# Sliding-window attention and a token-mixing MLP on one core: a new order of the work, six output buffers, first pieces in two parts, last stores tile by tile

## The chip, the cores and the metric

The kernel runs on one core of a Trainium2 chip. The metric is the device time of one execution in microseconds; the profiled execution also has a span, from its first to its last instruction. Engines are named PE (TensorE), DVE (VectorE), ACT (ScalarE), POOL (GpSimd) and SP (SyncE, which here only issues DMAs).

## What is computed

Attention over 576 positions with a window of 128, a linear position bias of its own for each of 8 heads, for 8 batches; its output then passes through a mixing layer, in which the tokens of a batch are mixed by a product of two projections:

```python
q, k, v: (8, 8, 576, 64)                      # batch, head, position, 64
scores = q @ k.T / 8 - slope[h] * |i - j|     # only 0 <= i - j < 128
x = softmax(scores) @ v                       # heads side by side: (8, 576, 512)
W_tok = (x @ w_q) @ (x @ w_k).T / 8           # (8, 576, 576)
out = relu(W_tok @ x) @ w_out                 # (8, 576, 512) float32
```

## The kernel before, in words

Everything is cut into some 735 small operations, and each is given an engine, PSUM banks and a place by one long list, `PLAN` (line 99). An item such as `36A0` is operation 36 on ACT with PSUM bank 0; P is PE, D is DVE, G is POOL, S is SP. `planned` (line 81) reads it. Every engine works through its own operations in exactly this order, so an operation that waits holds up all behind it on its engine. The list is written into the code; costs and due times given to each `op` are those that its planner used, and have no effect when the kernel runs.

The operations of a batch b, by name:

- `ld q`/`ld k` (two halves f of four heads each), `ld v` (five blocks of positions, the last one of 64): loads of 576 KB, 256 KB and 128 KB in float32, issued by SP (lines 392 and 427).
- `cast` (line 396, 431): float32 to float16, mostly on POOL; in batch 0 also on DVE and ACT. Each cast on POOL is made to wait for the last bias product M that stands before it in the list (the dependency named "port", line 698).
- `T` (line 399): 18 transposes of 64 x 64 on PE, then `evac` (line 408), which copies the result from PSUM to qT or kT, on ACT or DVE.
- `S` (line 445) and `E` (line 459): for a pair of heads c and a half u, the score products and their exponential (ACT, 128 x 1024). `M` (line 471, DVE) multiplies by the table of exponentials of the bias, zero outside the window.
- `PV` (line 488): 18 products with v, then `NR` (reciprocal) and `N` (scaling) on DVE, which write x.
- `XT`/`XTe` (lines 523, 534): 18 transposes of x and two copies; `WK`/`WKe`, `WQ`/`WQe`: the two projections and their copies; `G`/`Ge`: x weighted by one projection, summed over tokens, and its copy; `MX` (line 593) and `R` (line 600): the product with the other projection, and relu with the scale, written by two instructions to rm and rmt.
- `O` (line 623): four products with w_out for 128 positions, `Oe` (line 629) copies the result to an output buffer osb, and `st` (line 638) stores two such tiles, 512 KB. The last 64 positions of two batches go together: `OT`, `OTe` and `stt`, with buffers osbt.

In names such as S101 or O63 the first digit is the batch. Buffers are reused in rings whose lengths stand in `RINGS` (line 145): 8 for loads, 6 for casts of q and k, 3 for osb, 2 for osbt. The weights w_out and w_q, w_k are loaded through osb and osbt too (line 359).

At the start POOL and DVE make the identity, the masks and pads; ACT makes eight exponentials for the bias, DVE spreads them into a table (`table`, line 349). Nine operations `warm` (line 337) of four products of a matrix of ones with itself run on PE, into PSUM banks that nothing reads: eight of them first, and the ninth in batch 1.

Before the change, the early orders are (SP, ACT, PE, and DVE, cut):

```
SP   k00 q00 k01 q01 k10 v04 q10 v03 v01 v00 v02 k11 q11 w2 w3 k21 k20 v10 v14 q21 v11 v12 v13 q20
ACT  8 exps, cast k00, cast q00, evac q00, E011 E000 E001 E010 E031, cast v04, E030, evac q10, E021 E020, cast v02, E101 E100, evac q11, evac k11
DVE  table0 table1, evac k00 k01 q01, M00, evac k10, cast v03, M01 M03, cast v00 v01, M02, NR00 N00
PE   8 warm, T k00, T q00, S011, T k01, S001 S000, T q01, S010, T k10, S031 S021 S030 S020, T q10, PV00 PV01 S101 S100 PV02 PV03, T k11, T q11
end of PE   XT71 O61 XT73 O60 WK7 WQ7 G7 O62 MX72 MX71 MX70 MX73 O63 O72 O73 O71 O70 OT3
```

Of the kernel before, what the change touches and what calls it, by code (L numbers as in the profile page):

```python
# [9 lines left out]
FP32 = mybir.dt.float32  # L10
# [5 lines left out]
P = 128  # L16
# [16 lines left out]
class Op:  # L33
# [3 lines left out]
    def __init__(self, engs, name, prio, fn, reads=(), writes=(), after=(), opens=None, psum=None,  # L37
                 mode="F", dma=0.0, lag=0.0):
        self.engs, self.name, self.prio, self.fn = engs, name, prio, fn
        self.reads, self.writes, self.after = list(reads), list(writes), list(after)  # L40
        self.opens, self.psum, self.mode, self.dma, self.lag = opens, psum, mode, dma, lag
        self.deps, self.room, self.memory = {}, set(), {}
        self.banks = self.eng = self.place = None
        self.insts = []


def link(ops, rings):
# [4 lines left out]
    for o in ops:  # L52
        for r in o.writes:
            writers.setdefault(r, []).append(o)
        for r in o.reads:
            readers.setdefault(r, []).append(o)
# [24 lines left out]
def planned(ops):  # L81
# [3 lines left out]
    for item in PLAN.split():  # L85
# [4 lines left out]
        if o.opens:  # L90
# [9 lines left out]
1G 6D 39S 4D 0G 35S 2D 7D 47S 3G 8P0 5D 43S 14P0 20A 65S 19A 11P0 23A 59S 18A 12P0 17A 61S 24A 25D  # L100
21A 9P0 57S 22A 40A 15P0 53S 26D 13P0 51S 10P0 55S 36A 41P2 73S 42D2 69S 37P0 31S 38A0 48G 33S
250P0 99S 49P2 251A0 44G 245P4 91S 50D2 243P6 77S 244A6 45P0 248P2 66G 46D0 246A4 249A2 67P6 247D
260P0 255P4 261A0 258P2 62G 68D6 60A 253P0 259A2 58D 63P6 252D 64A6 256A4 262D 254A0 52D 54D 56A
257D 85S 403P0 95S 406P2 79S 404D0 74G 405D0 265P4 81S 263P6 266A4 407D2 83S 408D2 411P0 70G 87S
264A6 414P4 412D0 413D0 117S 75P2 32G 71P6 29S 415D4 34G 409P0 416D4 72A6 27S 410D0 113S 417P4
76A2 268P6 100G 418D4 270P0 269A6 280P2 267D 101P4 281A2 273P6 92G 102D4 274A6 531P2 78G 271A0
532D2 278P6 93P4 86G 275P2 279A6 272D 535P0 94A4 96G 533P1 536D0 276A2 534D1 80G 537P4 539P0 277D
111S 97P2 538A4 16P6 125S 98A2 82G 540D0 109S 84G 105S 282D 103S 427P0 419P2 107S 88G 428D0 121S
295P4 420D2 429D0 422P6 296A4 143S 421D2 293P0 118G 89P4 294A0 423D6 424D6 430P2 90A4 431D2 30G
541P0 425P6 432D2 542A0 283P4 426D6 433P2 284A4 28G 288P0 434D2 285P6 286A6 297D 290P4 547P2 289A0  # L110
543P6 287D 545P3 544A6 300P0 114G 546D3 291A4 119P6 548D2 549P3 120D6 301A0 126G 298P4 550A3 115P0
292D 127P6 299A4 650P2 110G 128D6 116A0 645P3 106G 651A2 112G 137S 557P0 646D3 553P4 104G 643P2
139S 554A4 558D0 133S 108G 644A2 135S 302D 435P0 131S 438P2 129S 122G 436D0 310P4 439D2 440D2
648P6 147S 311A4 647S 437D0 303P2 144G 649A6 123P4 304A2 124D4 138G 145P0 446P6 146A0 308P2 140G
447D6 448D6 443P4 309A2 555P0 444D4 441P6 134G 445D4 556A0 141P2 142A2 442D6 449P0 305P4 136G
450D0 306A4 551P6 313P2 552D6 559P0 314A2 132G 307D 315P4 163S 318P6 316A4 320P2 157S 655P1 130G
560D0 151S 319A6 451P4 159S 321A2 663P0 148G 195S 452D4 453D4 177S 323P6 664A0 312D 325P2 165S
149P4 656A1 161S 563P0 324A6 322D 169S 326A2 561P1 155S 317D 652S 454P6 564A0 462P2 150A4 164G
455D6 562D1 653P0 463D2 152G 456D6 459P4 654A0 464D2 660P1 160G 657S 460D4 158G 461D4 173S 153P2
661A1 328P6 189S 154D2 658P0 329A6 196G 203S 330P4 191S 659D0 565P6 333P2 331A4 199S 566D6 178G  # L120
457P0 334A2 465P4 458D0 197P6 466D4 198A6 338P0 166G 571P2 572D2 340P4 339A0 573P6 327D 341A4
575P7 162G 574D6 335P0 569P2 567P4 336A0 170G 577P6 568D4 570A2 576D7 156G 179P0 578D6 167P2 180A0
171P4 332D 467P6 168A2 666P0 337D 172A4 668P1 468D6 469D6 470P2 667A0 669A1 579P4 471D2 581P6
472D2 174G 580A4 673P0 670S 582A6 662S 585P2 342D 175P4 185S 586A2 345P6 671P1 346A6 183S 190G
674D0 181S 478P2 204G 176A4 672D1 187S 348P6 479D2 207S 480D2 475P0 349A6 192G 350P4 476D0 583P2
477D0 351A4 473P6 200G 474D6 481P0 584A2 343P4 482D0 344A4 353P6 355P2 352D 587P0 356A2 683P1
588D0 354A6 347D 678P0 684A1 186G 193P2 679A0 358P4 194D2 360P6 359A4 591P0 184G 361A6 357D 215S
201P2 205P4 209S 202A2 589P1 182G 592D0 221S 681P6 590D1 206A4 217S 188G 211S 362D 491P0 682A6
233S 483P2 225S 492D0 486P4 484D2 216G 493D0 676P6 208G 487D4 485D2 686P7 210G 677A6 488D4 680S
597P0 687A7 370P2 598D0 213S 494P4 371A2 222G 675S 593P6 495D4 373P0 594A6 496D4 241S 489P2 374A0  # L130
229S 380P6 490D2 218G 497P4 665S 498D4 381A6 223P2 375P0 212G 224D2 365P4 237S 376A0 601P6 235S
366A4 603P7 602D6 685S 377D 363P0 239S 599P2 368P4 364A0 605P6 600D2 226G 369A4 604D7 595P0 606D6
234G 227P2 596A0 219P4 372D 378P6 220A4 696P0 214G 228D2 379A6 694P1 697A0 367D 613P4 607P2 609P6
608A2 689P0 610A6 382D 507P2 614A4 691P6 690A0 242G 508D2 509D2 695A1 499P4 230G 692A6 611P0 500D4
383P2 501D4 612A0 693S 502P6 384A2 688S 238G 231P0 503D6 504D6 510P4 232A0 698S 709P2 236G 511D4
512D4 385P0 505P6 386A0 400P4 506D6 701P3 401A4 710D2 240G 398P0 702D3 513P6 711S 399A0 393P4
514D6 699P2 394A4 402D 615P3 700A2 395P0 616D3 388P4 703S 396A0 390P6 387D 617P2 389A4 619P3 618D2
397D 391A6 515P0 706P2 620A3 516D0 392D 621P4 625P6 622A4 704P3 517D0 707A2 626D6 518P4 705A3
627P0 519D4 708S 523P6 520D4 628A0 623P2 524D6 526P0 624A2 525D6 521P4 527D0 528D0 714P2 522D4
529P0 715A2 712P3 530D0 629P2 713D3 631P0 630D2 716S 633P1 632D0 717P0 634A1 639P2 637P4 635P6  # L140
640A2 638D4 641P2 636D6 719P1 642A2 718D0 727P2 720D1 729P3 728A2 721S 724P2 730A3 731S 722P3
725A2 732P2 723A3 726S 733A2 734S
# [3 lines left out]
         "wkn": 2, "wqT": 2, "g": 2, "rm": 8, "rmt": 8, "osb": 3, "osbt": 2, "inv": 3}  # L146
# [96 lines left out]
def steps(nc, pool, pp, q, k, v, moe_w_q, moe_w_k, moe_w_out, out):  # L243
# [24 lines left out]
    osb = [sb([P, 2, DM], FP32, f"osb{i}") for i in range(3)]  # L268
    osbt = [sb([P, DM], FP32, f"osbt{i}") for i in range(2)]
# [65 lines left out]

    for i in range(9):
        def f_warm(eng, bk):
            for _ in range(4):
                nc.tensor.matmul(bank(bk[0])[:, 0:P], ones, ones, start=True, stop=True)
        op({"PE": 0.45}, f"warm{i}", -98 + i, f_warm, reads=[("ident", 0)],  # L340
           opens=(f"warm{i}", 1))

# [31 lines left out]
    for i in range(4):  # L374
        r = [("osb", i - 3) if i < 2 else ("osbt", i - 4)]
        op({"SP": 0.6}, f"ld w{i}", (20, 20, 8, 8)[i], lambda eng, bk, i=i: f_ldw(eng, bk, i),
           writes=r, dma=1.4 if i < 2 else 0.7)
        op({"POOL": 1.04 if i < 2 else 0.33}, f"cast w{i}", (24, 24, 12, 12)[i],
           lambda eng, bk, i=i: f_castw(eng, bk, i), reads=r, writes=[("w", i)])
# [5 lines left out]
    for b in range(NB):  # L385
        for f in range(2):
            for x in range(2):
# [26 lines left out]
                op({"SP": 0.6}, "ld " + name, base - 14, f_load, writes=[("ld", i)], dma=1.65)  # L414
                op({"POOL": 1.12} if b else {"POOL": 1.12, "DVE": 1.15, "ACT": 1.0},
# [25 lines left out]
    for b in range(NB):  # L441
        for c in range(4):
            base, n = b * PERIOD + c * SLOT, 4 * b + c
            for u in range(2):
# [14 lines left out]
                def f_exp(eng, bk, n=n, u=u):  # L459
# [6 lines left out]
                   reads=[("qT", 2 * b + c // 2), ("kT", 2 * b + c // 2)],  # L466
# [13 lines left out]
    for b in range(NB):  # L480
        for c in range(4):
# [61 lines left out]
            op({"DVE": 0.74}, f"XTe{b}{c}", prio + 2.0, f_xte, psum=key,  # L543
# [3 lines left out]
    for b in range(NB):  # L547
# [35 lines left out]
        op({"DVE": 0.41}, f"WKe{b}", base + 3.0, f_wke, psum=f"WK{b}", writes=[("wkn", b)])  # L583
        op({"PE": 0.56}, f"WQ{b}", base + 4.0, f_wq, reads=r_xT + [("w", 2)],
           opens=(f"WQ{b}", 1), mode="C")
        op({"DVE": 0.41}, f"WQe{b}", base + 4.5, f_wqe, psum=f"WQ{b}", writes=[("wqT", b)])
# [31 lines left out]
    for b in range(NB):  # L618
        base = b * PERIOD + 6 * SLOT
        for t in range(4):  # L620
            n = (b * 4 + t) // 2

            def f_out(eng, bk, b=b, t=t):
                for db in range(4):
                    r = slice(256 * (t // 2) + t % 2, 256 * (t // 2) + 256, 2)
                    nc.tensor.matmul(bank(bk[0]), rm[:, b % 2, db, r],
                                     wout_sb[:, db, :], start=(db == 0), stop=(db == 3))

            def f_oute(eng, bk, t=t, n=n):
                copy(eng, osb[n % 3][:, t % 2, :], bank(bk[0]))  # L630
# [5 lines left out]
               writes=[("osb", n)])  # L636
            if t % 2:
                def f_store(eng, bk, b=b, t=t, n=n):
                    nc.sync.dma_start(
                        out=out[b, P * (t - 1) : P * (t + 1), :].rearrange("(p t) d -> p t d", t=2),  # L640
                        in_=osb[n % 3])
                op({"SP": 0.6}, f"st{b}{t}", base + t * SLOT + 1.6, f_store, dma=1.45,
                   reads=[("osb", n)])
        if b % 2:
# [7 lines left out]
            def f_outte(eng, bk, pr=pr):  # L652
                copy(eng, osbt[pr % 2], bank(bk[0]))

            def f_storet(eng, bk, pr=pr):
                for i in range(2):
                    nc.sync.dma_start(out=out[2 * pr + i, 512:576, :],
                                      in_=osbt[pr % 2][64 * i : 64 * i + 64])
# [72 lines left out]
```

## Time and profile before

| | |
|---|---|
| time, median of 4 runs | 150.74 us (149.59 to 152.04) |
| time of the profiled execution | 150.81 us |
| its span | 149.1 us |
| busy: PE, DVE, ACT, POOL | 125.4, 125.5, 118.5, 58.7 us |
| one exponential (64 of them, ACT) | 1.036 us |
| one bias product M (32, DVE) | 1.293 us |
| one cast of a q or k piece on POOL | 1.146 us |
| one copy of a q or k piece from PSUM: ACT, DVE | 1.12 and 1.36 us |
| one copy of an O tile: ACT, DVE | 0.606 and 0.685 us |
| from issue to landing: 512 KB store, 128 KB store | 4.3 and 3.2 us (median) |
| bytes moved by DMA | 39.4 MB |

Busy time says how much work an engine has; a stretch in which no engine is nearly always busy is one in which in-order queues wait for one another. A matmul's time in the records is its passage through the array; matmuls overlap, so a row of several is shorter than the sum of its parts. The list of idle times before a group names what came last.

### The profile page before, as it was taken

The numbers are of one execution on the slowest core, as the hardware profiler recorded it, in microseconds if no ns is written. First come the engines' busy times: TensorE is split into PE (matmuls) and PEld (weight loads), VectorE is DVE, ScalarE is ACT, GpSimd is POOL, SyncE is SP. The second block draws the span as 40 slices with busy tenths as digits, with TensorE's granted clock in tenths as the row PEclk, the third lists the DMA queues.
The fourth block names the chain that finished last, engine by engine and source line by source line (L and its number), as shares of the span: only waits on it lengthen the run. The fifth ranks groups of instructions, "written<-read, shape, count | busy, mean of one in ns | idle before, by whom it ended". The sixth has DMA issues, their size and how long they took to land.

```text
span 149.1 us, 5314 instructions
## 1 busy us (share of the span) xinstructions
PE 125.4 (84%) x2308; PEld 81.8 (55%) x2308; DVE 125.5 (84%) x212; ACT 118.5 (79%) x170; POOL 58.7 (39%) x78
## 2 busy tenths in 40 slices
PE   6568368776889968989989998999899999999870
PEld 6445266555756446647466566566644757555320
DVE  5739987979999996979999989999999989994700
ACT  6958947995889868997699999968999989741560
POOL 4054236454826756433936372365342710000000
PEclk9999968999999999999999999999999999999999
DMA  4999999999997999999999999589999975033075
GB/s 140 390 347 256 230 323 350 252 181 349 394 286 157 298 284 228 298 291 327 349 361 321 345 390 239 129 232 318 299 359 288 328 257 190 4 141 145 0 316 176
DMA packets 50775, 39.40 MB, mean 264 GB/s; under 512 B 39488, under 2 KB 39488, under 8 KB 50752
## 3 DMA queue, kind: packets, MB, share of 16 engines
q1 hardware_dynamic: 50752, 39.07, 88.9%
q8 instruction: 18, 0.29, 0.8%
q14 instruction: 5, 0.04, 0.1%
HBM read 29.62 MB, written 9.44 MB: 262 GB/s over the span
## 4 chain that ended last, share of the span: by engine, by line
PE 51%; DVE 21%; ACT 14%; DMA 6%; POOL 2%; SPq 1%; issue 1%; DVEq 0%; POOLq 0%
PE bank L159 51%; ACT pt L159 8%; DMA ld<-in_k_dram 6%; DVE pt L159 5%; DVE x L159 4%; DVE xT L159 3%; DVE kT L159 3%; POOL nat L159 2%; ACT qT L159 2%; ACT kT L159 2%; DVE osb L159 1%; SPq L159 1%; DVE rm L159 1%; DVE qT L159 1%; ACT rm L159 1%
## 5 line engine op out<-in xcount | busy, mean ns | idle before, releaser
L159 ACT ACTIVATE pt<-bank 128x1024 f16<-128x1024 f32 x64 | 62.7, 1036 | 9.2 <-PE bank L159 8.8
L159 POOL CAST nat<-ld 128x1152 f16<-128x1152 f32 x30 | 34.1, 1146 | 34.1 <-PE bank L159 12.4
L159 DVE TENSOR_TENSOR pt<-pt,table 128x2048 f16<-128x2048 f16 x32 | 40.9, 1293 | 1.5 <-ACT pt L159 1.5
L159 PE MATMUL bank<-wout_sb,rm 128*128 128x512 f16 x128 | 31.8, 380 | 0.0
L159 POOL CAST vt<-ldv 128x512 f16<-128x512 f32 (+1 forms) x35 | 20.8, 613 | 24.9 <-DVE pt L159 15.0
L159 PE MATMUL bank<-qT,kT 64*128 64x256 f16 (+2 forms) x320 | 25.5, 268 | 3.8 <-ACT qT L159 1.5
L159 PE MATMUL bank<-vt,pt 128*128 128x65 f16 x576 | 23.1, 197 | 4.8 <-ACT pt L159 3.1
L159 DVE TENSOR_TENSOR x<-bank,inv 128x640 f16<-128x640 f32 x32 | 25.8, 817 | 0.8
L159 PEld LDWEIGHTS <-pt 128*128 128x128 f16 x576 | 20.8, 100 | 9.9 <-issue 2.9
L159 PEld LDWEIGHTS <-kT 64*128 64x128 f16 x320 | 14.3, 100 | 10.5 <-issue 7.8
L159 ACT COPY osb<-bank 128x512 f32<-128x512 f32 x24 | 13.9, 606 | 7.1 <-PE bank L159 7.1
L159 PE MATMUL bank<-ident,nat 64*128 64x64 f16 x576 | 14.6, 199 | 5.5 <-ACT nat L159 1.6
L159 PEld LDWEIGHTS <-nat 64*128 64x128 f16 x576 | 12.0, 100 | 10.4 <-POOL nat L159 5.5
L159 PEld LDWEIGHTS <-rm 128*128 128x128 f16 x128 | 10.7, 98 | 12.6 <-issue 2.5
L159 ACT COPY qT<-bank 128x1152 f16<-128x1152 f16 x12 | 13.4, 1121 | 1.5 <-PE bank L159 1.5
L159 ACT ACTIVATE rm<-bank 128x512 f16<-128x512 f32 x21 | 12.7, 610 | 2.2 <-PE bank L159 2.2
L159 DVE COPY kT<-bank 128x1152 f16<-128x1152 f16 x8 | 10.8, 1353 | 3.0 <-PE bank L159 3.0
L159 DVE COPY xT<-bank 128x640 f16<-128x640 f16 (+1 forms) x32 | 12.5, 449 | 0.4 <-PE bank L159 0.4
L159 PE MATMUL bank<-x,wkn 128*64 128x512 f16 x80 | 10.1, 383 | 0.0
L159 ACT COPY kT<-bank 128x1152 f16<-128x1152 f16 x8 | 9.1, 1138 | 1.1 <-PE bank L159 1.1
L159 PE MATMUL bank<-wqT,gm 64*128 64x256 f16 x64 | 8.4, 288 | 1.5 <-DVE wqT L159 0.6
L159 DVE RECIPROCAL inv<-bank 128x10 f32<-128x10 f32 x32 | 6.7, 212 | 3.6 <-PE bank L159 3.2
(45 smaller groups left out, 113.0 us busy)
## 6 DMA issues: line engine op xcount, KB each, us to landing
ld<-in_k_dram SPq DMA_DIRECT2D x16, 576.0 KB, 7.1
ld<-in_q_dram SPq DMA_DIRECT2D x16, 576.0 KB, 7.4
ldv<-in_v_dram SPq DMA_DIRECT2D x32, 256.0 KB, 6.5
out_dram<-osb SPq DMA_DIRECT2D x16, 512.0 KB, 4.3
ldv<-in_v_dram SPq DMA_DIRECT2D x8, 128.0 KB, 6.3
osb<-in_moe_w_out_dram SPq DMA_DIRECT2D x2, 512.0 KB, 6.9
out_dram<-osbt SPq DMA_DIRECT2D x8, 128.0 KB, 3.2
osbt<-in_moe_w_q_dram SPq DMA_DIRECT2D x1, 128.0 KB, 6.6
```

What stands on the lines that cost most here:

```text
L159: r = call(*a, **k)
```

## The change

The ring of output buffers goes from 3 to 6 and that of the tail's from 2 to 3. The first two pieces, q00 and k00, are cast in two parts (5 and 4 of the 9 blocks) on two engines, and copied from PSUM in two parts, one for each pair of heads, so that the scores of one pair need only their part. Copies XTe, WKe and WQe may be given to ACT as well as to DVE. The last batch's output is stored tile by tile, 256 KB each, and its tiles take 128 rows that lie side by side. The nine `warm` operations are gone. With that, the whole list is a new one: 732 operations in another order, with another division of the work between ACT, DVE and POOL.

```diff
-RINGS = {..., "osb": 3, "osbt": 2, "inv": 3}
+RINGS = {..., "osb": 6, "osbt": 3, "inv": 3}
...
-    for i in range(9):
-        def f_warm(eng, bk):
-            for _ in range(4):
-                nc.tensor.matmul(bank(bk[0])[:, 0:P], ones, ones, start=True, stop=True)
-        op({"PE": 0.45}, f"warm{i}", -98 + i, f_warm, reads=[("ident", 0)],
-           opens=(f"warm{i}", 1))
...
+                if i < 2:
+                    for z in range(2):
+                        js = (slice(0, 5), slice(5, 9))[z]
+                        def f_cast(eng, bk, t=t, n=n, js=js):
+                            copy(eng, n[:, js], t.rearrange("p i (j d) -> p j i d", j=9)[:, js])
+                        def f_evac(eng, bk, x=x, z=z):
+                            dst = (qT, kT)[x][0][:, z, 0:S]
+                            copy(eng, dst.rearrange("p (g j) -> p g j", j=9),
+                                 bank(bk[z]).bitcast(F16)[:, 0:S].rearrange("p (j g) -> p g j", j=9))
...
-                   reads=[("qT", 2 * b + c // 2), ("kT", 2 * b + c // 2)],
+                   reads=([(f"qT.{c}", 0), (f"kT.{c}", 0)] if b == 0 and c < 2
+                          else [("qT", 2 * b + c // 2), ("kT", 2 * b + c // 2)]),
...
-            op({"DVE": 0.74}, f"XTe{b}{c}", ...
+            op({"DVE": 0.74, "ACT": 1.05}, f"XTe{b}{c}", ...
-        op({"DVE": 0.41}, f"WKe{b}", ...
+        op({"DVE": 0.41, "ACT": 0.36}, f"WKe{b}", ...
-        op({"DVE": 0.41}, f"WQe{b}", ...
+        op({"DVE": 0.41, "ACT": 0.36}, f"WQe{b}", ...
...
-                    r = slice(256 * (t // 2) + t % 2, 256 * (t // 2) + 256, 2)
+                    r = (slice(256 * (t // 2) + t % 2, 256 * (t // 2) + 256, 2) if b < NB - 1
+                         else slice(P * t, P * t + P))
...
-                copy(eng, osb[n % 3][:, t % 2, :], bank(bk[0]))
+                copy(eng, osb[n % RINGS["osb"]][:, t % 2, :], bank(bk[0]))
...
+            if b == NB - 1:
+                def f_store(eng, bk, b=b, t=t, n=n):
+                    nc.sync.dma_start(out=out[b, P * t : P * t + P, :],
+                                      in_=osb[n % RINGS["osb"]][:, t % 2, :])
```

What the new list does, read out of it by name. Early and late orders:

```
SP   k00 q00 q01 k01 q10 v04 k10 q11 k11 v01 v00 v03 v02 q20 v11 v12 w3 v14 k20 v13 v10 w2 k21 q21
ACT  8 exps, cast k00.1, cast q00.1, evac k00.1, evac q00.1, E011 E001 E000 E010, cast v04, E021 E020 E031 E030, evac q11, evac k11, cast v00 v03 v02, E100 E101
DVE  table1, cast k00.0, table0, evac k00.0 q00.0 q01 k01, M00, evac q10, M01, evac k10, cast v01, M03 M02, NR00 N00
POOL cast q00.0 q01 k01 q10 k10 (behind M00) q11 k11 (behind M01) q20
PE   T k00, T q00, S011 S001 S000, T q01, T k01, S010, T q10, S021 S031 S020 S030, T k10, T q11, T k11, PV00 S100 S101 PV01 PV02
end of PE   PV73 O53 PV71 G6 WQ6 XT71 XT73 MX63 O50 O51 WK7 MX60 MX61 MX62 WQ7 G7 O60 MX71 MX70 MX72 O61 O63 MX73 O62 OT3 O73 O70 O72 O71
end of SP   v71 v73 v74 v72 v70 st23 st31 st33 st43 st21 st41 stt2 st53 st51 st61 st63 stt3 st73 st70 st72 st71
```

Who does what, where it differs (operations in the whole kernel):

| | before | after |
|---|---|---|
| XTe | DVE 16 | DVE 13, ACT 3 |
| WKe | DVE 8 | DVE 2, ACT 6 |
| WQe | DVE 8 | DVE 3, ACT 5 |
| R | ACT 21, DVE 11 | ACT 22, DVE 10 |
| Oe | ACT 24, DVE 8 | ACT 22, DVE 10 |
| casts of v on ACT, DVE | 2, 3 | 4, 1 |
| casts of k00 and q00 | ACT 2 whole | DVE 1, POOL 1, ACT 2 parts |
| evac | ACT 20, DVE 12 whole | ACT 18, DVE 12 whole, and 2 parts each |
| stores st | 16 | 18 |

## The prediction

> **What bounds the kernel now.** I read the page's first two parts, then the busy time by stretch, the chain that ended last, the timeline of the first 30 us and of the last 20, and the groups by form for durations.
>
> ```profile
> PE 125.4 (84%) x2308; PEld 81.8 (55%) x2308; DVE 125.5 (84%) x212; ACT 118.5 (79%) x170; POOL 58.7 (39%) x78
> ```
>
> Three engines have nearly the same work, so no single one is "the" bound; where time is lost must be read by stretch. The columns are the length, then busy time of PE, PEld, DVE, ACT, POOL, the clock and the DMA share:
>
> ```profile
> 0.00:21.10 21.10, 12.46 (x203) 9.72 (x204) 15.18 (x29) 16.72 (x23) 6.33 (x13) 0.98 0.93 278
> 21.10:40.00 18.90, 14.99 (x366) 11.87 (x364) 16.80 (x28) 14.38 (x17) 11.70 (x15) 0.94 1.06 304
> 40.00:50.00 10.00, 8.75 (x170) 5.53 (x170) 9.96 (x14) 9.52 (x14) 5.16 (x6) 1.00 1.01 244
> 50.00:60.00 10.00, 8.20 (x197) 5.56 (x197) 8.67 (x16) 7.45 (x12) 6.81 (x10) 1.00 1.12 268
> 60.00:130.00 70.00, 67.12 (x1231) 42.05 (x1228) 66.31 (x111) 63.55 (x93) 28.72 (x37) 1.00 0.94 282
> 130.00:145.07 15.07, 13.93 (x156) 7.08 (x153) 8.59 (x18) 6.90 (x15) 0.00 (x0) 1.00 0.35 142
> ```
>
> From 60 to 130 PE is busy 96%, DVE 95%, ACT 91%: little is left there. From 21.1 to 60 it is 82, 91 and 81%: that is where a better order can win. The chain (start, us, what) says the same: a DMA at first, mixed engines with DVE from 33.8 to 51, PE alone at the end:
>
> ```profile
> 2.83 9.25 DMA ld<-in_k_dram
> ...
> 33.83 1.37 DVE pt L159
> ...
> 110.12 27.95 PE bank L159 x454
> 138.07 0.02 issue
> 138.09 0.60 ACT rm L159
> 138.69 0.12 ACT rmt L159
> 138.81 0.04 issue
> 138.85 5.62 PE bank L159 x26
> 144.47 0.02 issue
> 144.49 0.58 ACT osbt L159
> ```
>
> The execution profiled took 150.81 us for a span of 149.1: 1.7 lie around the span. The median of the runs is 150.74, so the sum needs no shift.
>
> **Idle products.** 32 end at 1.44 + 3.60 = 5.04, 1.24 us before the first transposes could start; four more sit at 34.22 in a hole that lasts to 35.98. Cover: PE has nothing to do there. Price 0; if they warmed the clock, they would be missed. They did not:
>
> ```profile
> 1.44 3.60 PE L159 MATMUL bank<-ones 128*128 128x128 f16 x32 [1.44 <-POOL ones L159]
> 6.28 0.66 PE L159 MATMUL bank<-ident,nat 64*128 64x64 f16 x18 [1.24 <-ACT nat L159]
> 27.54 0.43 PE L159 MATMUL bank<-ident,nat 64*128 64x64 f16 x18
> ```
>
> Eighteen transposes take 0.66 us right after the products and 0.43 at 27.5; 112 ns each is the products' own pace throughout. The granted clock reads 1.00 there, but the durations are those of the stretch from 20.0 to 23.4, where it reads 0.50 (ten score products: 1.03 at 21.98, 1.04 at 10.40). I take 0, with 0 to +1.4 as bounds (had the first six transposes run at 0.43, they would lose six times 0.23; fewer instructions in a hole can't cost).
>
> The Trainium skill, "TensorE: Matmul & The Clock Gate", section "Why this matters for your kernels", speaks against this edit: it wants 4 us or more of continuous products before timed work, to release the gate. By that rule the removal would cost half of one 3.4 us window, an estimate of 1.7 us; the rows above show 3.6 us of products that released nothing.
>
> **First pieces in two parts, and the order around them.** Before, ACT casts k00 and q00 whole (1.142 each) from 5.09 to 7.28, copies q00 from 8.03 to 9.15, and the first exponential starts at 9.85. After: DVE casts 5/9 of k00 behind one table (to about 6.1; 0.42 x 640/512 = 0.53), ACT the rest of k00 and then of q00 (0.62 each, from the 512-element cast), POOL 5/9 of q00 from its landing at 6.0 (0.64 to 0.77). T k00 at 6.15, T q00 at 6.9, half copies of 0.66 on ACT and 0.70 on DVE, first exponential at 8.9: 0.95 earlier. Whether this reaches PV00, the first value product, is another matter. By the landing events of the trace six loads land 1.5 us apart (4.5, 6.0, 8.6, 10.2, 12.0, 14.2) and v pieces about 0.9 apart. Now q11 and k11 go ahead of four v pieces, so v02 lands at 18.0 + 2 x 1.55 = 21.1. Then PV00 waits on ACT's order: eight exponentials end at 18.75; the cast of q11 on POOL waits, by the port rule in the code, for M01, which stands behind the copy of q10 on DVE and ends at 17.4; cast k11 to 19.7, T k11 to 20.4, copies of q11 and k11 on ACT to 21.55, casts of v00, v03, v02 (0.62 each) to 23.4. The reciprocal NR00 starts at 24.2, against 21.10 before: 3.1 us later. In return both transposes of batch 1 (0.70) and two ACT copies are done by then. Unknown: the half copies, 0.48 to 1.36 by the rows of 640- and 1152-element copies; they touch the first exponential only, not NR00.
>
> The skill's "Advanced Engine Details and Errata", section "VectorE Performance Modes", says that DVE's second port is GpSimd's too, and the two block each other. No POOL cast of before lies beside a table copy; the new cast of q00 does. An estimate by the rule: up to 1.1 us, which takes the early start away and leaves the later steps as they are.
>
> **Work moved between engines.** DVE loses 3 XTe (0.482 + 0.415 each), 6 WKe (0.485), 5 WQe (0.475), one relu (0.684 + 0.215) and two v casts (0.422): 9.7. It gains 2 Oe (0.685), two half copies (0.70) and the cast (0.53): 3.3. Net -6.4: 119.1. ACT gains 3 XTe and 11 WKe/WQe, which it never did before: by a line through its 64- and 512-element copies of PSUM (0.239, 0.610) and the 1152-element one (1.12), 1.33 and 0.45 each (bounds: DVE's 0.90 and 0.485; 1.7 and 0.61), 4.0 + 5.0; plus one relu 0.85 and two v casts 1.24; minus two Oe 1.21, and 1.0 and 0.9 for the halves. Net +7.9 (5 to 11): 126.4. PE loses 4.0 of idle products. ACT becomes the engine with the most work.
>
> **Output buffers and stores.** No engine's wait in the list of waits is put down to a store, so three more buffers free no engine: 0. SP waited 24.8 us for output copies (14.4 ACT, 10.4 DVE) with loads queued behind it; these go, since stores 23 to 63 now stand behind the last load. POOL, 39% busy, covers late loads today; if that cover went, each late piece would cost its 7 us landing less what is prefetched. The stores left for the end are ten of 512 KB; at 1.4 us each they need 14 us, and O5 to O7 reuse their slots from about 130 on: hidden, if the last load is out by 115. If it is not, a copy waits for a store's landing, 4.3 us each time. SP issues two stores more (0.5 each, in its own idle time). In the last batch's O products the weights are read row by row and not every second row: the same 16 loads, 0.
>
> **The end.** Before, 4.03 us follow the last copy: two issues (1.11) and a landing of 3.2. After, one issue of 256 KB: 0.55 less, and a landing between 3.2 (128 KB) and 4.3 (512 KB), so 3.6: net -0.2 to -0.9, I take -0.4. The hole of 0.53 at 138.85, where O waits for the last relu, is covered by O61, O63 and O62 in the new order: -0.5.
>
> **Sum.** From NR00 to the last copy, before: 145.07 - 21.10 = 123.97 us for PE 112.99 + DVE 110.33 + ACT 101.80 = 325.1 of work, 2.62 per us. After NR00 remain PE 111.9 (112.99 - 0.40 - 0.70), DVE 119.1 - 16.3 = 102.8, ACT 126.4 - 18.3 = 108.1: 322.8. (Done by NR00: DVE's 15.18, with the cast 0.53 and two halves 1.40 more and two v casts 0.84 less; ACT's 16.72, less 1.04 for the casts, plus 0.2 for two half copies in place of one, 1.14 for copying q11 and k11 instead of q10, and 1.24 for two v casts.) At the same density 123.1 us: last copy at 147.3, span 147.3 + 3.6 = 150.9. Then density: the 98.7 of work from 21.1 to 60 took 38.9 us (2.54 per us). The new order brings batch 1's v earlier (last of five about 29 instead of 34.5, by the same landing spacing), so PV1 no longer waits at 35.98 (1.37 idle), and takes three copies off DVE where it is the chain. At the mean from 40 to 130 (249.5/90 = 2.77) that work takes 35.6: -3.3. With the hole, -0.5: span 147.1, time 148.8.
>
> **Rivals.**
> - *No denser.* The order wins nothing from 21 to 60, the late NR00 stays: 150.9 + 1.7 = 152.6, or 150.5 if half is won. For it: every early wait of before was one step of an in-order queue, and a new order has its own. Against it: 2.54 is plainly under 2.81 from 60 to 130.
> - *ACT paces (slower).* ACT has 108.1 left at NR00, some 9 in the last 14.6 us. If it is busy 89.5% of the rest, as from 40 to 130, that takes 99/0.895 = 110.6: last copy 149.4, time 154.7. It decides when ACT stays under 93% (last copy at 145.5 is break-even, 106.7 us for 99); my forecast needs 95%. Against it: the engine with most work reached 96% from 60 to 130. For it: no 40 us of before show ACT there.
> - *PE paces throughout.* Its 111.9 at 95.5%: last copy 141.4, time 146.7. It needs ACT at 96.5%, what PE alone reached.
>
> **How the numbers follow.** Forecast 50% (own range 146.9 to 150.1: 2.9 per us as from 80 to 90, or one third of the gain), no denser 22%, ACT 18%, PE 10%. A measurement of this kernel tells about 1% (149.2 and 152.2). Faster: 40 of the forecast's 50 and PE's 10, 0.50. Same: 10 of the forecast, 13 of no denser, 0.23. Slower: 9 and 18, 0.27. Range 146.2 to 153.6: it leaves out half of PE and of ACT, and a little of each other case.
>
> **What would show it.** First exponential near 8.9, NR00 near 24; transposes before 20 at 0.66 as before; ACT the busiest at about 126 and over 93% from 25 to 130; PE idle from 25 to 60 under 5 us; the last O products without a hole; 3.6 us after the last copy. I am wrong if NR00 comes near 21, if ACT's new copies take over 1.7 or under 0.9, if PE waits for output copies that wait for stores, or if the clock reads 0.5 after 30.

## The result, and the profile after

The changed kernel takes 149.87 us (median of 51 runs, 148.41 to 152.84), the kernel before 150.85 (median of 77 runs beside it). The ratio is 0.9955, with a 95% interval of 0.9938 to 0.9973: 0.45% faster, where 1.3% was forecast. Ratios here leave out, on both sides, executions that lie over 1.5% above the fastest of their kernel, so they are not always the quotient of two medians. The profiled execution took 149.87 us for a span of 148.2; 1.7 us lie around the span, as before.

The work by engine, in the page's first part:

```profile
PE 122.6 (83%) x2272; PEld 79.0 (53%) x2272; DVE 120.3 (81%) x196; ACT 124.0 (84%) x189; POOL 60.3 (41%) x79
```

and by stretch (length, then PE, PEld, DVE, ACT, POOL, clock, DMA share, GB/s):

```profile
0.00:21.10 21.10, 8.60 (x180) 6.49 (x182) 15.98 (x29) 15.21 (x23) 9.51 (x16) 1.00 0.92 283
21.10:40.00 18.90, 14.11 (x307) 10.93 (x302) 15.27 (x25) 15.28 (x19) 7.90 (x11) 1.00 1.04 283
40.00:50.00 10.00, 8.34 (x169) 5.17 (x168) 7.41 (x13) 8.74 (x14) 4.90 (x7) 1.00 1.10 303
50.00:60.00 10.00, 9.94 (x178) 5.73 (x177) 9.12 (x16) 8.90 (x14) 7.17 (x10) 1.00 1.11 274
60.00:130.00 70.00, 67.41 (x1327) 44.00 (x1327) 65.92 (x102) 66.36 (x102) 30.85 (x38) 1.00 0.92 270
130.00:145.07 15.07, 14.25 (x134) 6.72 (x126) 6.61 (x15) 9.47 (x22) 0.00 (x0) 1.00 0.49 186
```

Add PE, DVE and ACT in each row and hold it against the row of before. From 21.1 to 60, where the forecast put the gain, the three did 98.7 us of work before and 97.1 now (3.9 us of this stretch now lie ahead of the first reciprocal). From 60 to 130 they did 197.0 and now 199.7; from 130 to 145.07, 29.4 and now 30.3. So a good part of the gain lies after 60, where the forecast expected nothing but the last hole, and little of it before 60, where it expected 3.3 us. How much in each stretch is worked out at the end.

The chain that ended last (start, us, what) shows where the early time sits:

```profile
18.25 2.44 POOL nat L159 x2
...
20.74 0.68 PE bank L159 x18
...
21.44 1.12 ACT kT L159
22.56 1.57 ACT vt L159 x3
...
24.17 4.23 PE bank L159 x56
...
45.80 1.12 issue
...
106.69 37.57 PE bank L159 x535
...
144.29 0.58 ACT osb L159
```

The first rows are the predicted path to the first reciprocal: casts of q11 and k11 on POOL, T k11, the copy of k11, the casts of v on ACT, and only then products. "45.80 1.12 issue" is a stop in which PE waited for no other engine; the kernel before has two of this kind, of 0.45 us at 42.0 and 0.36 at 105.3. The end is as predicted: PE without a hole for 37.57 us, so the wait of 0.53 for the last relu is gone, and 3.3 us from the end of the last copy (144.87) to the end of the span, where it was 4.03.

### The profile page after: what moved, and what is told of

Its sections match the earlier page's. It is cut to its first block, busy times and chain, and to the rows that moved or that the text cites. A ratio compares the mean times of both kernels' runs of the same rounds, so it can differ in the third digit from the quotient of the medians.

```text
span 148.2 us, 5259 instructions
## 1 busy us (share of the span) xinstructions
PE 122.6 (83%) x2272; PEld 79.0 (53%) x2272; DVE 120.3 (81%) x196; ACT 124.0 (84%) x189; POOL 60.3 (41%) x79
## 4 chain that ended last, share of the span: by engine, by line
PE 51%; DVE 23%; ACT 19%; POOL 2%; issue 2%; POOLq 0%; DVEq 0%
PE bank L159 51%; ACT pt L159 7%; DVE pt L159 6%; DVE qT L159 4%; DVE x L159 3%; DVE xT L159 2%; DVE kT L159 2%; ACT kT L159 2%; ACT qT L159 2%; ACT rm L159 2%; DVE table L159 2%; ACT osb L159 2%; POOL nat L159 2%; ACT xT L159 1%; ACT table L159 1%
## 5 line engine op out<-in xcount | busy, mean ns | idle before, releaser
L159 POOL CAST nat<-ld 128x1152 f16<-128x1152 f32 (+1 forms) x31 | 35.0, 1138 | 34.6 <-DVE pt L159 15.5
L159 DVE TENSOR_TENSOR pt<-pt,table 128x2048 f16<-128x2048 f16 x32 | 39.9, 1258 | 1.2 <-ACT pt L159 1.2
L159 POOL CAST vt<-ldv 128x512 f16<-128x512 f32 (+1 forms) x35 | 21.7, 644 | 17.3 <-DVE pt L159 13.1
L159 PE MATMUL bank<-vt,pt 128*128 128x65 f16 x576 | 24.0, 199 | 2.5 <-ACT vt L159 2.2
L159 PEld LDWEIGHTS <-pt 128*128 128x128 f16 x576 | 21.6, 101 | 7.9 <-issue 3.6
L159 ACT COPY qT<-bank 128x1152 f16<-128x1152 f16 (+1 forms) x11 | 12.1, 1097 | 1.2 <-PE bank L159 1.2
L159 ACT COPY kT<-bank 128x1152 f16<-128x1152 f16 (+1 forms) x9 | 9.6, 1066 | 3.9 <-PE bank L159 2.0
L159 DVE COPY osb<-bank 128x512 f32<-128x512 f32 x10 | 6.9, 686 | 5.8 <-PE bank L159 5.8
L159 DVE COPY xT<-bank 128x640 f16<-128x640 f16 (+1 forms) x26 | 10.3, 450 | 1.0 <-PE bank L159 0.9
L159 DVE COPY kT<-bank 128x1152 f16<-128x1152 f16 (+1 forms) x8 | 10.2, 1274 | 0.0
```

Of the source, the lines that this page charges most:

```text
L159: r = call(*a, **k)
```

## The experiments

Ratios are to the kernel before, run on the same chip. The kernels came in four sets, and the unchanged changed kernel stood at 0.9959 in the third and 0.9905 in the fourth, so what lies in different sets is compared to half a per cent at best. The first set (the first four kernels) and the second (pieces whole, halves free, early v and 33 products, each alone) have no such control, and the four of the second all stand at 0.981 to 0.988, lower than most of them were expected. "First exponential" and "first reciprocal" are their starts in the profiled execution; "clock full from" comes from the trace's records of the granted clock.

### Parts of the change, added to the kernel before, or undone

**No idle products (in the kernel before).**

```diff
-    for i in range(9):
+    for i in range(0):
         def f_warm(eng, bk):
```

> The kernel before with the 36 idle products gone and nothing else changed. My theory: they lie in holes of PE and open no clock, so the ratio to before is 1.000 (0.997 to 1.003), the first transposes stay at 0.66 us and the first exponential at 9.85. Rival, that they do warm the array: the first transposes and score products slow down further or the half clock lasts past 23.4, and the time rises by 0.5 to 1.7 us (ratio 1.003 to 1.011).

152.33 us, ratio 1.0033 [0.9987, 1.0078]. First exponential at 9.85, as before; first reciprocal 20.72. The price is 0 within what can be measured, as predicted.

**Six output buffers (in the kernel before, order unchanged).**

```diff
-RINGS = {..., "osb": 3, "osbt": 2, "inv": 3}
+RINGS = {..., "osb": 6, "osbt": 3, "inv": 3}
```

> The kernel before with six and three output buffers in place of three and two, its order unchanged. My theory: no engine's wait was put down to a store, so ratio 1.000 (0.997 to 1.003). Rival, that copies into the buffers did wait for stores in places that the list of waits puts down to something else: 0.5 to 1.5 us less (ratio 0.990 to 0.997).

152.47 us, 1.0033 [0.9990, 1.0076]. Buffers alone bring nothing. Its profiled execution (154.96 us) showed something else: the 32 idle products filled a step of the clock (3.41 us, see the last section) that ended at 4.9 us, the clock opened there, and went back to half one step later, after one in which PE was 30% busy. So the products can open the clock, if the edges of a step fall right, but they stand so early that little runs faster for it.

**Last stores tile by tile (in the kernel before, with OT3 ahead of O72).**

```diff
-            if t % 2:
+            if b == NB - 1:
+                op({"SP": 0.6}, f"st{b}{t}", ...)
+            elif t % 2:
 end of PLAN: OT3 O72 O73 O71 O70, stores stt3 st72 st63 st73 st71 st70
```

> The kernel before with the last batch stored tile by tile, its tiles of rows that lie side by side, and the last tail tile moved ahead of the last four tiles; all else as before. My theory: from the last copy to the end of the span 3.3 to 3.6 us instead of 4.03, time lower by 0.4 to 0.7 us (ratio 0.995 to 0.997). Rival, that the last landing is bound by what else is being written: nothing gained, ratio 1.000.

153.16 us, 1.0079 [1.0033, 1.0125]: slower, where 0.4 to 0.7 us less was expected. The end of this kernel, SP's issues and the last copy:

```profile
143.33 1.12 SPq L158 DMA_DIRECT2D out_dram<-osbt  x2
144.54 3.53 SPq L158 DMA_DIRECT2D out_dram<-osb  x5
...
146.17 0.58 ACT L158 COPY osb<-bank 128x512 f32<-128x512 f32 x1 [0.28 <-PE bank L158]
```

Seven stores are issued in 4.7 us, to 148.07, though the last copy ends at 146.75: st63 had been put behind st72, and SP now paces the end, 4.6 us from last copy to span end (4.03 before). More, smaller stores did not shorten the end where SP still had an older store to issue; in the changed kernel it has none. But the end is 0.6 us of it only: the last copy itself ends 1.7 us later than before (146.75 for 145.07). That is lost between 30 and 57 us, ahead of anything that the edit touches, in an execution in which the clock went to half from 37.0 to 40.5. So the slower time says little about the stores.

**Copies XTe, WKe and WQe back on DVE (in the changed kernel).**

```diff
 14 items of PLAN: XTe (3), WKe (6), WQe (5)
-A
+D
```

> The changed kernel with all copies XTe, WKe and WQe given back to DVE (14 of them), its order otherwise as it is. If the moved copies carry the gain: DVE rises to about 128.5 us and ACT falls to about 115, DVE becomes the chain and the time rises by 1.5 to 3 us (ratio to the kernel before 1.005 to 1.016). Rival, that the division of work matters little as long as PE has the longest chain: ratio stays at 0.995 (0.992 to 0.998).

152.16 us, 1.0050 [1.0002, 1.0099], against 0.9955 for the change as it is: in this order, the moved copies are worth about 1% (1.4 us; half a per cent more or less, as the set has no control), more than the whole change. A list planned anew around DVE might lose less; that was not tried. The row for 60 to 130 us:

```profile
60.00:130.00 70.00, 65.20 (x1292) 42.23 (x1291) 66.88 (x109) 62.35 (x88) 29.54 (x38) 1.00 0.92 274
```

It does 194.4 us of work there, the changed kernel 199.7. DVE is busy 96% and ACT 89%. From 60 us to the last copy PE, DVE and ACT together do 2.64 us of work per us, in the changed kernel 2.71, before 2.66: the gain after 60 goes with the copies.

**Last stores in pairs again (in the changed kernel).**

```diff
-                    r = (slice(256 * (t // 2) + t % 2, ...) if b < NB - 1 else slice(P * t, P * t + P))
+                    r = slice(256 * (t // 2) + t % 2, 256 * (t // 2) + 256, 2)
```

> The changed kernel with its last four tiles stored in pairs of 512 KB again (and taking every second row again). My step: from the last copy to the end of the span 3.9 to 4.4 us instead of 3.33, time 0.4 to 1.0 us above the changed kernel. Rival, that the last landing is what counts and is the same: no difference.

150.34 us, 0.9982 [0.9939, 1.0025]; the unchanged control of its set 149.88, 0.9959 [0.9914, 1.0005]. In the profile 4.4 us follow the last copy, as expected (3.9 to 4.4), where the changed kernel and its controls have 3.3. The difference in time, 0.2% or 0.5 us at the medians, has the predicted sign and is not resolved.

### The start

**First pieces cast and copied whole (in the changed kernel).**

```diff
-                    for z in range(2):
-                        js = (slice(0, 5), slice(5, 9))[z]
+                    for z in range(1):
+                        js = slice(0, 9)
```

> The changed kernel with q00 and k00 cast whole on ACT and copied whole (k00 on DVE, q00 on ACT), as in the kernel before. Its two halves were seen to run one behind the other on two engines, so I expect the split to bring little: first exponential within 0.7 us of 10.5, NR00 within 0.5 of 25, ratio to the kernel before 0.994 to 0.999. Rival, that the split is what carries the gain of the change: ratio 1.000 to 1.005.

149.59 us, 0.9875 [0.9817, 0.9932]; first exponential 9.77, first reciprocal 24.15, against 10.54 and 24.97 for the changed kernel. Both come earlier than expected, and the ratio lies under the expected range; the rival, that the split carries the gain, is out. The split, as it was built, makes the start later. The timeline of the changed kernel shows why (columns: start, us, engine, line, operation, out<-in, count, idle time before and its releaser):

```profile
7.76 0.74 DVE L159 COPY kT<-bank 128x576 f16<-128x576 f16 x1
8.43 0.74 DVE L159 COPY qT<-bank 128x576 f16<-128x576 f16 x1
8.54 0.64 ACT L159 COPY kT<-bank 128x576 f16<-128x576 f16 x1 [1.85 <-DVE kT L159]
9.21 0.64 ACT L159 COPY qT<-bank 128x576 f16<-128x576 f16 x1
...
10.54 1.02 ACT L159 ACTIVATE pt<-bank 128x1024 f16<-128x1024 f32 x1 [0.70 <-PE bank L159]
```

The two halves were to run side by side; ACT's begins when DVE's has ended, with DVE's copy named as what it waited for. They read different PSUM banks and write different columns, but of the same tile, and were kept in order; the next kernel shows that nothing but the declared order did it.

**The two halves made free of each other.** This says to the scheduler that they touch different columns:

```diff
+    for n in ("q00", "k00"):
+        tc.declare_no_dep(by_name[f"evac {n}.1"].insts[0], by_name[f"evac {n}.0"].insts[0], ...)
```

> The changed kernel with the second half of each first copy no longer waiting for the first half (they read different PSUM banks and write different columns). If this wait is what keeps the early start from arriving: first exponential at 8.6 to 9.3 instead of 10.54, M00 about 1.3 us earlier, NR00 near 23.7, and the time lower by 0.3 to 1.3 us (ratio to the kernel before 0.987 to 0.994). Rival, that the start is paced by the landings and by ACT's order: NR00 stays at 24.5 to 25 and the ratio at 0.994 to 0.997.

148.67 us, 0.9818 [0.9761, 0.9875]; first exponential 9.24, first reciprocal 23.91. It was run again beside a control:

> The two half copies of the first q and k decoupled. If the wait between them is what ate the gain of the split: the first exponential at 9.2 us and 1.1 to 1.3 us less than the control (148.7 us). If the earlier start is lost again before 50 us (clock, instruction packets): within 0.5 us of the control.

149.21 us, 0.9900 [0.9835, 0.9965]; the control 149.70, 0.9905 [0.9860, 0.9951]. Its timeline:

```profile
7.17 0.64 ACT L159 COPY kT<-bank 128x576 f16<-128x576 f16 x1 [0.55 <-PE bank L159]
7.69 0.74 DVE L159 COPY kT<-bank 128x576 f16<-128x576 f16 x1
...
9.23 2.85 ACT L159 ACTIVATE pt<-bank 128x1024 f16<-128x1024 f32 x3 [0.88 <-PE bank L159]
```

The wait between the halves is real: without it the first exponential is 1.3 us earlier and the first reciprocal 0.8 (24.13 against 24.91 in the control). The time follows by 0.5 us at the medians, not by 1.3, and the ratios can't be told apart. That is the rival's case: at the 25th exponential the two kernels are level again (56.25 us, the control 56.23), after stops of PE of 0.21 and 0.83 us at 38.9 and 44.7, where the control has one of 0.55. So this wait is not the main part of what is missing.

**Batch 1's q11 and k11 loaded and used later, so that v comes first.** SP `v04 k10 v01 v00 v03 v02 q11 k11 q20`; ACT casts v ahead of copying q11 and k11; PE `PV00 S100 S101 PV01 T q11 PV02 T k11 S120`. Alone, and with the halves made free:

```diff
 SP in PLAN
-v04 k10 q11 k11 v01 v00 v03 v02 q20
+v04 k10 v01 v00 v03 v02 q11 k11 q20
```

> The changed kernel with the v pieces of batch 0 loaded ahead of q11 and k11, cast on ACT before the copies of q11 and k11, and the transposes of q11 and k11 moved behind PV01 and PV02. If the late first value product costs time: NR00 comes near 22 instead of 24.97 and the time falls by 1 to 2.5 us (ratio to the kernel before 0.979 to 0.989). Rival, that the delay is hidden because ACT or PE paces everything later and does the same work anyway: NR00 near 22, but ratio 0.993 to 0.998 as in the changed kernel.

> The changed kernel with both edits: v pieces of batch 0 ahead of q11 and k11, and the second half of each first copy free of the first. If the late first value product costs time by itself: NR00 near 21, time 1.5 to 2.5 us under the changed kernel. Rival, that an earlier PV00 only lengthens the stretch of half clock (it lasted to 37.0 with the first edit alone): NR00 near 21, half clock to 30 or later, time within 0.7 us of the changed kernel.

149.69 us, 0.9884 [0.9825, 0.9942], and 148.98 us, 0.9899 [0.9856, 0.9943]. The first reciprocal comes at 21.79 and 20.68, 3.2 and 4.3 us earlier than in the changed kernel. The first lies in the range of its theory, but in the set without a control. The second gains 0.9 us on the control of its set (149.88), less than the 1.5 to 2.5 of its theory. In its profile the clock stays at half until 35.5 us (30.0 in that control's): four steps of 3.41 us in a row with PE busy 85, 80, 85 and 94% did not open it; the next one, at 100%, did. And 4.3 us follow its last copy, not 3.3, for which the runs show no cause. Up to the last copy (142.64 us) it leads that control (144.97) by 2.3 us and the control of the fourth set (143.88) by 1.2. So of a reciprocal that comes 4.3 us earlier (the late one is the step on which the forecast spent most of its working) about half at most reaches the last copy.

### The clock

**33 idle products in the gaps of PE between 15 and 21 us (in the changed kernel).** In the profile below they run between 17.4 and 22.0 us.

```diff
+    for i, c in enumerate((14, 5, 14)):
+        def f_warm(eng, bk, c=c):
+            for _ in range(c):
+                nc.tensor.matmul(bank(bk[0])[:, 0:P], ones, ones, start=True, stop=True)
 PE in PLAN: T k10, warm0, T q11, warm1, T k11, warm2, PV00
```

> The changed kernel with 33 idle products put into PE's holes between the transposes of k10 and PV00. If the half clock until 28.1 us costs time: the clock opens by 21 to 25, PV00 to PV02 run at 0.72 instead of 1.1 us each and the time falls by 0.5 to 1.4 us (ratio to the kernel before 0.986 to 0.992). Rival, that these products wait for other engines anyway: ratio 0.994 to 0.998.

148.84 us, 0.9810 [0.9752, 0.9869], in the set without a control, where the kernel with the halves free stands at 0.9818 with no products. Again, beside the control:

> 33 idle products in the gaps of TensorE between 15 and 21 us. If half a clock from 20 to 28 us is what ate the gain: clock full for one window more before 28 us, 1 to 2 us less than the control. If not: within 0.5 us of it, or slower by the products' own 2 us at half the clock.

148.23 us, 0.9818 [0.9743, 0.9893], 1.5 us below the control (149.70, 0.9905 [0.9860, 0.9951]). The two ratios overlap, as both carry the spread of the kernel before; held against each other, the means of the runs that count in them differ by 1.4 us, 0.9 either way at 95%. Of this, the two profiles show 0.8 us inside the span (last copy at 143.09 and 143.88). The first products with v in the changed kernel, and in this one:

```profile
23.13 0.54 PE L159 MATMUL bank<-vt,pt 128*128 128x65 f16 x7 [1.74 <-ACT vt L159]
24.17 0.77 PE L159 MATMUL bank<-vt,pt 128*128 128x65 f16 x11 [0.49 <-ACT vt L159]
```

```profile
22.80 0.37 PE L159 MATMUL bank<-vt,pt 128*128 128x65 f16 x7 [0.84 <-ACT vt L159]
23.83 0.49 PE L159 MATMUL bank<-vt,pt 128*128 128x65 f16 x11 [0.67 <-ACT vt L159]
```

Seven products take 0.54 and 0.37 us, eleven 0.77 and 0.49: the first pair is on half a clock. The column of the clock reads 1.00 for both kernels in that stretch: here the clock had opened at 18.7 us; in the changed kernel the trace's first record comes only when the clock opens, at 28.1, and before it the column says nothing. The durations tell. The first part of the stretch from 21.1 to 60 us, in the control and in this kernel:

```profile
21.10:40.00 18.90, 14.53 (x324) 11.42 (x319) 15.24 (x25) 15.53 (x20) 7.88 (x11) 1.00 1.06 286
```

```profile
21.10:40.00 18.90, 15.56 (x352) 11.98 (x353) 16.06 (x27) 16.23 (x20) 9.49 (x13) 0.91 1.09 287
```

Up to 60 us this kernel does 47.85 + 26.53 + 28.43 = 102.8 us of work, 0.9 of it idle products, the control 45.30 + 26.98 + 28.26 = 100.5. Here too the clock went to half for one step, at 32.4 us.

**The same products with the halves free.** Both edits above.

> Both together. If the two causes are separate and both real, their gains add: about 2.2 to 2.5 us less than the control (147.5 us). If both only move the same wait (the first output batch waits for the loads of v), the sum is that of the better one alone: 148.5 us.

148.21 us, 0.9779 [0.9670, 0.9888], span 146.0, clock full from 17.4 us to the end in the profiled execution. It is the best version found: 2.2% under the kernel before (1.1 to 3.3), and 1.5 us under the control. Against the products alone the medians agree; that the two gains add is not shown.

**Early v, halves free and products 9/18/10.**

> The same two edits, and 37 idle products in holes of PE (9 behind the score products S010, 18 behind the transposes of k10, 10 behind those of k11). If the half clock is what ate the early start: full clock from 17 to 24 on, PV products at 0.72 us, time 2 to 3.5 us under the changed kernel and 1 to 2 under the same edits without products. Rival, that later stretches pace the end whatever the start does: within 0.7 us of the changed kernel.

149.59 us, 0.9818 [0.9730, 0.9905]; runs from 147.18 to 150.81. In the profiled execution the clock opened first at 17.4 us and went back to half three times, each time for one step: at 20.8, 31.1 and 44.7, after steps in which PE was 49, 57 and 44% busy. That the earlier work is lost there is a guess. No better than the products alone, and inconclusive as to the order; the control of its set has 149.88.

### The controls

> The changed kernel itself, unchanged, as the measure for the other three of this group on the same chip: ratio to the kernel before 0.985 to 0.998.

149.88 us, 0.9959 [0.9914, 1.0005].

> Control: the changed kernel as it is, beside the next three. 149.9 us, 0.995 to 0.997 of the kernel before; first exponential 10.5 us, first reciprocal 25.0 us, clock full from 28.1 us on, in every theory.

149.70 us, 0.9905 [0.9860, 0.9951], a ratio under the expected one; exponential, reciprocal and clock (10.49, 24.91, 28.2) came as expected. Its profiled execution has a span of 147.2, 1.0 less than the first one of the very same kernel, and yet took 149.77 us: 2.6 us lie around this span, 1.7 to 1.9 around those of the other 17 profiles. What makes the difference is not shown; where spans are compared with this control, up to 0.9 us can be that. PE's stop near 45 us, in the first and in this one:

```profile
46.93 0.30 PE L159 MATMUL bank<-xT,wq_sb 128*64 128x320 f16 x1 [1.12 <-issue]
```

```profile
45.58 0.29 PE L159 MATMUL bank<-xT,wq_sb 128*64 128x320 f16 x1 [0.55 <-issue]
```

The page's list of queues has one of instructions, q8, with 17 packets of 16 KB. Those of this stretch come some 6 us apart (in the first execution they end at 38.6, 45.3 and 50.8). The 18 traces of this study hold 26 stops of PE of 0.2 us and more after the start that the profile puts down to "issue", and every one of them ended 1.2 to 1.8 us after the end of such a packet: in the control the packet was done 1.3 us sooner than in the first execution (44.0), and the stop was half as long. From there on the control leads by 1.3 us at the 25th exponential (56.23 for 57.58) and by 1.0 at the last copy. That PE waited for its instructions is read off these times; no run changed the packets. What makes a packet late (all loads and stores together ran at 303 GB/s from 40 to 50 us, at 244 before) was not tried.

## Why the prediction was wrong, point by point

The sum was 1.1 us too low: span 148.2 for 147.1, time 149.87 for 148.8. It splits so: first reciprocal at 24.97 for 24.2, +0.8; from there to the last copy 119.9 us for 119.3, +0.6; after the last copy 3.3 for 3.6, -0.3. That the middle term is no further off is luck: the density up to 60 us, on which the gain was to rest, fell short by 2.5 us, and an unforeseen gain after 60 (1.1 us) and less work than forecast (0.8 us) made up for most of it.

- *Idle products, 0.* Right. The rule of the Trainium skill that was weighed there ("TensorE: Matmul & The Clock Gate", "Why this matters for your kernels": warm up with 4 us or more of matmuls) would by the forecast's estimate have had 1.7 us lost; leaving them out cost 0.3% with an interval that holds 0. But the rule was dropped too quickly: the same kind of products, put right before the work that was to run fast, are worth about 1.4 us.
- *The start, exponential at 8.9 and reciprocal at 24.2.* The path was right, step for step. (The landings are not 1.5 us apart throughout, as was said: by the six times given they are 1.5 to 2.6. v02 landed at 21.8 for 21.1, ahead of its cast all the same.) The exponential came at 10.54: the half copies ran one after the other. The decoupled kernel has 9.23 and 24.13, and so this one wait is the whole 0.8. The other danger named, the port that DVE shares with POOL ("Advanced Engine Details and Errata", "VectorE Performance Modes"), shows too: four table copies take 1.51 us beside the cast of q00 and 1.17 without, and two products M 3.29 beside casts, where two means make 2.5. That is 0.3 us ahead of the first exponential, where the forecast's estimate by that page was up to 1.1, and 0.8 later on, off the path to the reciprocal. That the port is the cause is the page's account; no run here tests it.
- *Work moved: DVE 119.1, ACT 126.4.* Measured 120.3 and 124.0; ACT's copies cost 0.46 for a WKe or WQe and 1.30 for an XTe, where 0.45 and 1.33 were estimated. ACT's total is 2.4 lower all the same because the busy time counts overlapping records once: the durations of its instructions add up to 8.7 us more than before, the busy time to 5.4 more. So from the first reciprocal on there was 112.4 + 102.5 + 105.9 = 320.8 us to do, where 322.8 was forecast. ACT became the busiest, as said, but was busy 92% from 25 to 130, not over 93%.
- *Buffers 0, the end -0.4, the last hole -0.5.* Right: -0.7 at the end, and no hole. The last load was out at 113, inside the stated limit of 115.
- *Density, -3.3 from 21 to 60 us.* This is the step that failed: "At the mean from 40 to 130 (249.5/90 = 2.77) that work takes 35.6". From the first reciprocal to 60 us the engines did 30.74 + 30.01 + 30.07 = 90.8 us of work in 35.03, 2.59 per us. At the 2.54 of before this takes 35.8: won 0.8, not 3.3. In the control, with shorter stops of PE, it is 94.4 in 35.09, 2.69 per us, and 2.1 won. What held it down: PE ran on half a clock until 28.1, where the kernel before had it open for good from 23.5, and had stops of 0.61 and 1.12 us at 40 and 46. The two executions of the same kernel, which differ in their stops, are 1.3 us apart; the products, with the clock open before 20 us, took about 1.4 us off the time. With both edits of the best version the stretch from its first reciprocal carries 2.72, still under 2.77. How the shortfall divides between clock, stops and the order itself stays open. The forecast's signs could not warn of this: it named a clock at half after 30, where 23.5 was the limit, and PE idle under 5 us from 25 to 60, which came true (4.3), since a PE on half a clock counts as busy.
- *Nothing after 60 but the hole.* From 60 us to the last copy the engines did 2.71 per us against 2.66 before, worth 1.6 us (1.1 in the control) where 0.5 was forecast; with the copies back on DVE it is 2.64 and the time 152.16. The forecast treated the stretch from 60 to 130 as full, because PE was busy 96% and DVE 95%. Taking 5 us of work off DVE let more be done there; that DVE paced the stretch is an inference, since its share hardly changed (95 and 94%) and only ACT's rose, from 91 to 95%.

Of the rivals, "no denser" was nearly right up to 60 us and wrong in the total (152.6), since it saw no gain after 60; its milder form, half of the gain won, gave 150.5. "ACT paces" did not come true: ACT was under the 93% that was to decide it, but had 2.2 us less to do than forecast, and reached 95% from 60 to 130. "PE paces throughout" (146.7) was not reached by any version; the best stands at 148.2.

## What to carry to other kernels

A stretch in which two engines are 95% busy can still be shortened: here moving 14 copies from DVE to ACT was worth about 1%. Price such a move there too, not only in the thin stretches. Work per us is compared from the same operation on, here the first reciprocal; fixed times mix a late start with a thin stretch. When an order is made sparser for PE, ask when the clock will now open, and read it from the durations of a repeated operation, not from the clock's column. Two halves of a copy on two engines are parallel only when nothing orders them: look at what the second one's wait is put down to.

## What the runs showed of the hardware

- The granted clock changes at steps of 3.41 us (in the kernel before it opened at 16.65, went to half at 20.07 and opened again at 23.48), whose phase differs from execution to execution: three executions of the changed kernel opened at 28.1, 28.2 and 30.0. In the 18 traces it opened after steps in which PE was busy 86 to 100%, and stayed at half after others of up to 94%. It went to half after steps of 9 to 65%, and stayed open after others from 56% on; so these runs show no sharp bound. A long gap is not needed: it also went to half after steps of 30 to 65% in which PE had no gap over 1.9 us.
- PE can stop for its own instructions, up to 1.84 us at a time (at 41.36, in the kernel with early v, free halves and products), and the clock can go to half with it: that step was 44% busy, and the clock went to half at its end.
